# Blocks 2 and 3 on their way down: seven block products for eight, partial sums joined from SBUF, and first products that go on in the second's bank

## The chip, the cores and the metric

The kernel runs on one core of a Trainium2 chip. The metric is the device time of one execution in microseconds; lower is better. Engines are called as in the profile: PE is TensorE (with PEld, its weight loads), DVE is VectorE, ACT is ScalarE, POOL is GpSimd, SP is SyncE, whose queue issues the DMAs. Blocks, pairs and passes are counted from 0.

## What is computed

```python
for c in range(nc):                       # chunks of 32 queries, 16 keys more on the left, 8 on the right
    k_full = np.concatenate([mem_k, k[:, :, l_start:r_end]], axis=2)      # 8 memory keys
    v_full = np.concatenate([mem_v, v[:, :, l_start:r_end]], axis=2)
    scores = scale * np.matmul(q[:, :, c_start:c_end], k_full.transpose(0, 1, 3, 2))
    a = np.exp(scores - np.max(scores, axis=-1, keepdims=True))
    a = a / (np.sum(a, axis=-1, keepdims=True) + 1e-09)
    attn[:, :, c_start:c_end] = np.matmul(a, v_full)
x = attn.transpose(0, 2, 1, 3).reshape(3072, 512)       # batch 4, 8 heads, 768 tokens, 64 wide
h = x @ w_in                                            # 512 -> 2048
g = np.maximum(h, 0.0) + alpha * np.minimum(h, 0.0)
out = g @ w_out                                         # 2048 -> 512
```

## The kernel before

Everything is float32. A float32 product is made of three matmuls of a rounded type: each operand is kept as a high part (`xh`, `gh`) and a low part (`xl`, `gl`), and low x high, high x low and high x high add up in one PSUM bank. A high part is a cast on ScalarE, a low part a subtraction on VectorE ("split" below).

The 3072 tokens are eight blocks of 384 (`BT`), the 2048 features 16 slices of 128 (`NF`), the 512 inputs four parts of 128. A slice is multiplied upward into a bank `h_ps`, bent on ScalarE and VectorE (`g`), split, and multiplied downward into `o_ps`. Attention runs between these products in twelve events: score products `s_ps`, softmax on VectorE, ScalarE and POOL (`e`), eight transposes on VectorE (`pt`), value products `a_ps`.

- Blocks 0 and 1 go plainly (`hidden`): 12 upward matmuls of 384 columns a slice, 9 downward of 512 columns with the activations as the stationary operand.
- Blocks 2 and 3 go plainly for slices 0 to 7. Block 2's partial sum is put aside in HBM (`put_aside`), block 3's stays in its banks.
- Pass 0 (`whole`) takes slices 8 to 15 of blocks 2 and 3. Upward, two token blocks times two slices times two halves of the input make eight block products; sums of blocks of `x` and of the weights turn them into seven (a Strassen-Winograd scheme). Downward it multiplies plainly again, onto block 3's banks and into new ones for block 2, to which the part put aside is added (`put`).
- Passes 1 and 2 (`deep`) take blocks 4 and 5, then 6 and 7, with all 16 slices in eight pairs. They use seven products upward and downward: six matmuls of 384 columns a product. The sums of activations (`less`) are POOL's, the splits VectorE's (`gs`), the results are collected by `begun` (first part, copied out of the bank) and `ended` (second part, added).

The weights' sums are made by POOL, ScalarE and VectorE, split, stored to HBM (`w_all`, `w_two`) and loaded again before each product into a ring of ten slots (`w_p`) by SP's queue. `w_low` holds slices 0 to 7 of `w_out` plainly for passes 1 and 2. `make` builds the combinations of blocks 2 and 3 for pass 0, `transform` those of a later pass.

No engine's order is written down as such: each operation is a `step` with a cost, what it reads and writes, and a rank (`rest`, the work that still follows). A list scheduler fixes the order of every engine before the run; `MOVED` shifts the rank of single steps. An engine works its list in order, so what stands behind a waiting operation waits too.

Of the kernel before, what the change touches and what calls it, by code (L numbers as in the profile page):

```python
# [47 lines left out]
def first_slice(p):  # L48
    return 0 if p else PLAIN


# [3 lines left out]

NTT = BT // P
NPW, NPROD = NF // 2, 7
# [42 lines left out]
for f in range(NF):  # L100
# [6 lines left out]
PAIR, PASS, SHORT, DUO = 4.7, 134.0, 78.0, 15.7  # L107

DEEP = 1
DEEP_PASS = 119.0  # L110
BEHIND = SHORT + (DEEP - 1) * PASS + (NPASS - DEEP) * DEEP_PASS

BEGIN = (19, 24, 28, 31, 36, 41)


LAST_BEGINS = ((0, 4), (0, 6), (0, 7), (1, 24), (1, 47), (1, 74), (1, 96))
# [3 lines left out]
MAKE = 40  # L120

EVENT_LEAD = 8.0
# [4 lines left out]
STARTS_LONG = [x + 1 for x in BEGIN if x >= FIRST_LONG - 1] + [len(ORDER)]  # L127
# [5 lines left out]
FIRST_SUMS, SUMS_PACE = 21, 3.5  # L133
SUMS_ORDER = (0, 4, 5, 6, 7, 3, 1, 2)
SAVE_ORDER = (3, 1, 2, 4, 5, 6, 7, 0)
FIRST_SAVE, EARLY_SAVES = 23, 6
LOAD_AHEAD = 20.0

OVER = 2


LEAD = 9.5
# [8 lines left out]
DUE_WEIGHTS = 4  # L151
# [142 lines left out]
def body(ctx: ExitStack, tc: tile.TileContext, qvw, kw, first, w_in, w_out, alpha, out, out_t):  # L294
# [66 lines left out]
    def begins(u):  # L361

        if u < NWIN:
            return u // NPAIR
        n = (u - NWIN) // 2
        if n < len(BEGIN):
            return BEGIN[n]
        p, x = LAST_BEGINS[n - len(BEGIN)]
        lead = DUO * (min(x, NPW) - first_slice(p) // 2) + 2.1 * max(0, x - NPW - first_slice(p))
        return len(ORDER) + (BEHIND - pass_start(p) + lead) / PAIR  # L370
# [435 lines left out]

    OKEYS = [("o", i) for i in range(NTT)]
    ROOMS = {"gh0": (0, None), "gl0": (1, 0), "gh1": (1, 1)}
# [17 lines left out]
    def hidden(blk, f, first_f, last_f):  # L826
# [5 lines left out]
        if place >= BEGIN[0] + 3:  # L832
            hk = ("h0", "h1", "a")[place % 3]
# [57 lines left out]

        def down(o_ps):
# [24 lines left out]
        def add_down(o_ps, rank=None, after=()):  # L917
            step(PE, 0.697 * NTT, partial(down, o_ps), reads=[("w", 1, f, 0), ("w", 1, f, 1), gh, gl],
                 writes=[("s", 0), ("s", 1), "a"] if joint else OKEYS,
                 rest=rest(down_at) if rank is None else rank, after=after)  # L920
# [38 lines left out]
    aside = hbm.tile([P, NTT * DM], F32, name="aside")  # L959

    def put_aside(blk, o_ps):

        for tt in range(NTT):
            n = NTT + next(ntmp) % 2
            o = {}

            def take(tt=tt, n=n, o=o):
                o["t"] = tmp.tile([P, DM], F32, name="o_t", tag=f"o{n}")
                nc.scalar.copy(out=o["t"], in_=o_ps[tt])

            def leave(tt=tt, o=o):
                nc.sync.dma_start(out=aside[:, tt * DM:(tt + 1) * DM], in_=o["t"])

            step(ACT, 0.59, take, reads=OKEYS, writes=[("tmp", n)], rest=rest(PLACE[blk, PLAIN - 1] + 1))
            step(SP, 0.75, leave, reads=[("tmp", n)], writes=[("aside", tt)])

    def bring_back():

        for n in range(4):
            k, x = 2 + n // 2, "hl"[n % 2]  # L980

            def load(n=n, k=k, x=x):
                t = home(("aside", n), lambda: xp.tile([P, BT], F32, name="part", tag=f"x{x}{k}{AT[k][2]}"))
                nc.sync.dma_start(out=t, in_=aside[:, n * BT:(n + 1) * BT])

            step(SP, 0.65, load, reads=[("aside", tt) for tt in range(NTT)], writes=[("part", n)],
                 after=[("x" + x, k, AT[k][2])], rest=pass_start(1) + 6.0)

# [5 lines left out]
    w_low = hbm.tile([NPW, P, 2 * DM], F32, name="w_low")  # L994
    staged = {}

    def keep_plain(q):
# [8 lines left out]

        def whole(f):
            nc.sync.dma_start(out=w_low[f].rearrange("p (x m) -> p x m", x=2), in_=ws[f, 1].bitcast(F32))

        if q >= NPW // 2:  # L1010
            for f in (f1 - NPW, f2 - NPW):
                step(SP, 1.3, partial(whole, f), reads=[("w", 1, f, 0), ("w", 1, f, 1)], writes=[("wl", f)])
# [4 lines left out]
    def keep_sums(q):  # L1017
# [21 lines left out]
        def low(n, i):  # L1039
            nc.gpsimd.tensor_tensor(out=staged["x"][n][:, 1], in0=part(i),  # L1040
                                    in1=staged["x"][n][:, 0].bitcast(F32), op=ALU.subtract)
# [22 lines left out]
        def end(j, i):  # L1064
            n = spots[j]
            step(POOL, 0.75, partial(low, n, i), reads=[("sm", i)], writes=[("sx", n)])
            step(SP, 0.65, partial(leave, n, j), reads=[("sx", n)], writes=[("wd", q, j)])
# [42 lines left out]
    def raw_after(p, k, t):  # L1110
# [3 lines left out]
        part = [("part", (k - 2) * 2 + t)] if p == 2 and k >= 2 else []  # L1114
        return [("x" + key[1], key[2], AT[key[2]][2])] + part
# [59 lines left out]
    def combo(p, j, kt, x):  # L1175
# [16 lines left out]
    def combo_after(p, j, kt, x):  # L1192
        if p == 0:
            f = PLAIN + ((MADE[j] * 2 + kt) * 2 + x) // 2
            return [("w", 0, f, y) for y in range(2)]
        f = 2 + ((j * 2 + kt) * 2 + x) // 5
        old = [("raw7", k) for k in range(NK)] if f == LAST_SLOT else [("g0", 14), ("g0", 15)] if f == SPARE else []
        return [("w", i, f, y) for i in range(2) for y in range(2)] + old
# [5 lines left out]
    def load_product(q, j, left, kind="wd"):  # L1204
# [7 lines left out]
        def load():  # L1212
            t = home(("ring", k), room)
            wring[r] = t[:, n]
            if low:
                nc.sync.dma_start(out=t[:, n].bitcast(F32),
                                  in_=w_low[f].rearrange("p (x m) -> p x m", x=2)[:, :, i * HALF:(i + 1) * HALF])
            else:
                nc.sync.dma_start(out=t[:, n].rearrange("p x m -> p (x m)").bitcast(F32),
                                  in_=(w_all if kind == "wd" else w_two)[q, j])  # L1220

        low = kind == "w2" and q < NPW // 2 and j in QUARTERS
        if low:
            f, i = 2 * q + QUARTERS[j][0], QUARTERS[j][1]
        step(SP, 0.65, load, reads=[("wl", f) if low else (kind, q, j)], writes=[("wr", r)],
             after=[] if isinstance(k, str) else [("w", k[1], k[0], 0), ("w", k[1], k[0], 1)], rest=left)
        return r

    def load_low(f):
        _, at_ = out_place(f)  # L1230

        def load():
            nc.sync.dma_start(out=ws[at_, 0].rearrange("p x m -> p (x m)").bitcast(F32), in_=w_low[f])

# [131 lines left out]
    def whole(p):  # L1366
# [185 lines left out]
        for d in late:  # L1552
            down(o1, ob, *d)
# [502 lines left out]
```

## Time and profile before

| | |
|---|---|
| time, median of 3 runs | 569.68 us (569.61 to 570.16) |
| the profiled execution | 569.56 us |
| its span on the core | 567.8 us |
| TensorE busy | 561.1 us, 99% of the span |
| VectorE, ScalarE, POOL busy | 436.8, 337.9, 301.5 us |
| granted TensorE clock | 1.00 in every stage (the level of 2.4 GHz) |
| DMA, mean over the span | 267 GB/s |

The profiled execution is 0.12 us below the median; its time is its span and 1.8 us around it. Stages, in us from the span's start: blocks 0 and 1 with the plain halves of 2 and 3 up to 243.1, pass 0 to about 317.4 (with some steps beyond), pass 1 upward to 384.5 and downward to 447.8, pass 2 upward to 506.0 and downward to 564.4.

### The profile page before, as it was taken

Reading aid. Unit: us, or ns where it says so; the run is one execution under the profiler, and the core shown is the slowest. Engines: PE = TensorE matmul, PEld = TensorE weight load, DVE = VectorE, ACT = ScalarE, POOL = GpSimd, SP = SyncE. Lnnn points to the kernel's source line nnn. Section 1 sums busy time; section 2 is a strip of 40 time slices with the busy share of each in tenths; the row PEclk is TensorE's granted clock in tenths of the full one; section 3 lists DMA queues with packets and bytes.
Section 4 is the critical chain, followed back from the end, with each engine's and each line's share of the span. In section 5 each row is a group of like instructions: output and inputs, shape, how many; then the busy total and the mean of one; then the engine's idle time right before and its main releaser. Section 6 shows DMA issues by size and latency. Waiting matters only on the chain.

```text
span 567.8 us, 14440 instructions
## 1 busy us (share of the span) xinstructions
PE 561.1 (99%) x5356; PEld 520.4 (92%) x5356; DVE 436.8 (77%) x732; ACT 337.9 (60%) x912; POOL 301.5 (53%) x350
## 2 busy tenths in 40 slices
PE   8999999999999999999999999999999999999997
PEld 5889899888989888989998899999999999999997
DVE  4888899984849668767593897799999677669951
ACT  3798888664653466646755766766386255555540
POOL 3530000069889799998886992218935022229400
PEclk9999999999999999999999999999999999999999
DMA  8999998456476358377997799889887987878784
GB/s 344 398 407 408 409 352 295 152 179 194 155 253 227 103 164 293 126 269 240 319 321 284 216 349 327 291 281 289 257 274 223 321 270 252 255 248 258 234 291 141
DMA packets 82342, 151.44 MB, mean 267 GB/s; under 512 B 8416, under 2 KB 29408, under 8 KB 82272
## 3 DMA queue, kind: packets, MB, share of 16 engines
q1 hardware_dynamic: 82272, 150.51, 78.1%
q8 instruction: 43, 0.70, 0.5%
q14 instruction: 27, 0.22, 0.1%
HBM read 112.99 MB, written 37.49 MB: 265 GB/s over the span
## 4 chain that ended last, share of the span: by engine, by line
PE 96%; DMA 3%; issue 0%; DVE 0%; SPq 0%
PE h_ps L1713 21%; PE o_ps L1816 21%; PE h_ps L869 18%; PE o_ps L898 18%; PE o_ps L1438 6%; PE h_ps L1381 5%; PE a_ps L549 3%; DMA early<-first 3%; PE s_ps L451 3%; PE a_ps L701 1%; PE o_ps L687 1%; PE s_ps L427 0%; DVE o_t L1842 0%; SPq L623 0%
## 5 line engine op out<-in xcount | busy, mean ns | idle before, releaser
L1713 PE MATMUL h_ps<-xs,w_p 128*128 128x384 f32 x672 | 118.6, 335 | 0.0
L1779 POOL TENSOR_TENSOR big<-big 128x384 f32<-128x384 f32 x64 | 73.5, 1177 | 84.1 <-DVE big L1737 75.1
L1713 PEld LDWEIGHTS h_ps<-xs,w_p 128*128 128x128 f32 x672 | 116.5, 188 | 0.8
L1816 PE MATMUL o_ps<-gs,w_p 128*128 128x384 f32 x576 | 102.4, 335 | 0.0
L1816 PEld LDWEIGHTS o_ps<-gs,w_p 128*128 128x128 f32 x576 | 100.0, 188 | 0.2
L869 PE MATMUL h_ps<-xh,w 128*128 128x384 f32 x384 | 97.9, 335 | 0.0
L1801 DVE TENSOR_TENSOR gs<-big,gs 128x384 fp32r<-128x384 f32 x96 | 82.0, 893 | 8.6 <-ACT gs L1798 8.1
L510 POOL TENSOR_TENSOR e<-e,den 128x384 f32<-128x384 f32 x24 | 23.9, 1016 | 101.2 <-DVE den L506 98.6
L869 PEld LDWEIGHTS h_ps<-xh,w 128*128 128x128 f32 x384 | 69.6, 188 | 1.0
L1798 ACT CAST gs<-big 128x384 fp32r<-128x384 f32 x96 | 48.8, 522 | 28.7 <-PE o_ps L1816 24.6
L869 PE MATMUL h_ps<-xl,w 128*128 128x384 f32 x192 | 65.7, 342 | 0.0
L531 DVE STREAM_TRANSPOSE pt<-e 32x384 f32<-32x384 f32 x96 | 54.6, 569 | 7.0 <-POOL e L510 5.3
L484 ACT ACTIVATE e<-s_ps,mx 128x64 f32<-128x64 f32 x144 | 43.9, 336 | 12.3 <-DVE mx L477 12.3
L898 PE MATMUL o_ps<-w,gh 128*128 128x512 f32 x156 | 48.6, 393 | 0.0
L898 PE MATMUL o_ps<-w,room 128*128 128x512 f32 x165 | 45.2, 393 | 0.0
L898 PE MATMUL o_ps<-w,gl 128*128 128x512 f32 x111 | 43.8, 395 | 0.0
L878 ACT ACTIVATE g<-h_ps 128x384 f32<-128x384 f32 x48 | 23.8, 498 | 33.5 <-PE h_ps L869 23.3
L869 PEld LDWEIGHTS h_ps<-xl,w 128*128 128x128 f32 x192 | 36.0, 188 | 2.0
L881 DVE SCALAR_TENSOR_TENSOR g<-g,rise,h_ps 128x384 f32<-128x384 f32 x48 | 28.9, 607 | 11.3 <-ACT g L878 10.8
L1721 ACT COPY big<-h_ps 128x384 f32<-128x384 f32 x48 | 23.2, 483 | 22.2 <-PE h_ps L1713 20.9
L898 PEld LDWEIGHTS o_ps<-w,room 128*128 128x128 f32 x165 | 30.8, 188 | 6.1
L1734 ACT ACTIVATE g<-h_ps 128x384 f32<-128x384 f32 x48 | 23.6, 494 | 18.9 <-DVE h_ps L1724 14.3
(139 smaller groups left out, 1084.9 us busy)
## 6 DMA issues: line engine op xcount, KB each, us to landing
w_p<-w_all SPq DMA_DIRECT2D x140, 256.0 KB, 3.8
w_p<-w_two SPq DMA_DIRECT2D x88, 256.0 KB, 3.2
v_t<-qvw SPq DMA_DIRECT2D x24, 384.0 KB, 4.4
w_t<-w_in SPq DMA_DIRECT2D x16, 512.0 KB, 10.1
w_t<-w_out SPq DMA_DIRECT2D x16, 512.0 KB, 9.4
w_all<-sums_x SPq DMA_DIRECT2D x32, 256.0 KB, 3.8
w_two<-two_x SPq DMA_DIRECT2D x32, 256.0 KB, 4.2
qk<-kw SPq DMA_DIRECT2D x24, 272.0 KB, 4.1
```

The source lines that it names most:

```text
L484: nc.scalar.activation(out=st["e"][:, i], in_=st["s"][h2][:, n], func=AF.Exp, scale=SCALE, bias=d["mx"][:, u - us[0], n, h2:h2 + 1], accum ...
L531: nc.vector.transpose(out=pt[row:row + CH, g % 2], in_=e_pair.rearrange("p u n k -> p (u n) k")[g * CH:(g + 1) * CH, :, half * CH:(half + ...
L869: nc.tensor.matmul(out=h["ps"][:, :BT], lhsT=ws[f, 0][:, wk, k * P:(k + 1) * P], rhs=ring[k][xk][AT[k][blk]], start=(k == 0 and n == 0), s ...
L881: nc.vector.scalar_tensor_tensor(out=h["g"], in0=h["g"], scalar=rise[:, f:f + 1], in1=h["ps"][:, :BT], op0=ALU.mult, op1=ALU.add)
L898: nc.tensor.matmul(out=o_ps[tt], lhsT=h[gk][:, tt * P:(tt + 1) * P], rhs=ws[f, 1][:, wk], start=(f == first_f and i == 0), stop=(f == last ...
L1381: nc.tensor.matmul(out=t[0][:, :BT], lhsT=wring[r][:, wk, kt * P:(kt + 1) * P], rhs=combo(p, j, kt, xk), start=first and kt == 0 and n == ...
L1438: nc.tensor.matmul(out=o[tt], lhsT=d[gk][:, tt * P:(tt + 1) * P], rhs=w[:, wk], start=f == (first_slice(p) if o is o2 else 0) and n == 0, ...
L1713: nc.tensor.matmul(out=t["t"][:, :BT], lhsT=wring[r][:, wk, kt * P:(kt + 1) * P], rhs=combo(p, j, kt, xk), start=first and kt == 0 and n = ...
L1779: step(POOL, 1.02, lambda: nc.gpsimd.tensor_tensor(out=quad(q, dst), in0=quad(q, a), in1=quad(q, b), op=ALU.subtract), reads=[key(q, a), k ...
L1798: nc.scalar.copy(out=hi(), in_=quad(q, i))
L1801: nc.vector.tensor_tensor(out=lo(), in0=quad(q, i), in1=hi().bitcast(F32), op=ALU.subtract)
L1816: nc.tensor.matmul(out=t["t"][:, :BT], lhsT=wring[r][:, wk, dd * P:(dd + 1) * P], rhs=parts[xk](), start=first and q == 0 and n == 0, stop ...
```

## The change

`whole` is gone, and `deep` serves pass 0 too, with pairs 4 to 7 alone (`first_pair`), so that slices 8 to 15 of blocks 2 and 3 go downward by seven products for eight. For this their slices 0 to 7 go downward with the weights as the stationary operand (`down_turned`): 12 matmuls of 384 columns a slice into four banks, the result turned. Block 2's partial sum goes to HBM in four pieces of 384 columns, block 3's is kept in SBUF (`keep_part`), and pass 0's `begun` and `ended` add the banks to both.

In every pass a first product that others build on is copied by ScalarE from its bank X into bank Y (`passed`), and the next product adds to Y in PSUM, where VectorE added a copy before; the order of the downward products changes for this. Ten operations of `make` and eight low parts of weight sums go from POOL to VectorE, the weights' sums are made in another order, `w_low` goes away, and the tables that place the attention's events and the moved steps are new.

```diff
+def first_pair(p):
+    return 0 if p else PLAIN // 2
...
-LAST_BEGINS = ((0, 4), (0, 6), (0, 7), (1, 24), (1, 47), (1, 74), (1, 96))
+LAST_BEGINS = ((0, 1), (0, 22), (0, 46), (1, 27), (1, 68), (1, 86), (1, 106))
...
-EVENT_LEAD = 8.0
+EVENT_LEAD = 24.0
...
+LOW_OUT = (0, 5)
+MAKE_DVE = (1,)
...
+        def down_turned(o_ps):
+            if f == first_f:
+                o_ps.extend(bank_tile(k, "o_ps") for k in TKEYS)
+            for fb in range(NFB):
+                for i, (wk, gk) in enumerate(((0, "gl"), (1, "gh"), (0, "gh"))):
+                    nc.tensor.matmul(
+                        out=o_ps[fb][:, :BT],
+                        lhsT=ws[f, 1][:, wk, fb * P:(fb + 1) * P],
+                        rhs=h[gk],
+                        start=(f == first_f and i == 0), stop=(f == last_f and i == 2),
+                    )
...
+    def keep_part(o_ps, clock):
+
+        for fb in range(NFB):
+            def take(fb=fb):
+                (nc.vector.tensor_copy if fb % 2 else nc.scalar.copy)(out=first_tile(4 * NPW + fb), in_=o_ps[fb][:, :BT])
...
+                (nc.vector if kt in MAKE_DVE else nc.gpsimd).tensor_tensor(out=rooms[r][0](), in0=get(a), in1=get(b), op=alu)
...
-    DOWN_ORDER = (0, 1, 2, 3, 5, 4, 6)
+    DOWN_ORDER = (0, 2, 3, 1, 4, 5, 6)
...
+        def passed(t, to, name):
+            def go():
+                to["t"] = bank_tile(to["k"], name)
+                nc.scalar.copy(out=to["t"][:, :BT], in_=t["t"][:, :BT])
+
+            act(0.48, go, [t["k"]], [to["k"]])
+
...
-                    if j == 0:
+                    if j == 0 and opening:
                         copied(t[i], q, 0)
+                    elif j == 0:
+                        passed(t[i], y[i], "h_ps")
                     elif j == 1:
-                        added(t[i], q, 0, True)
+                        if opening:
+                            added(t[i], q, 0, True)
                         bent(f1, q, 0, t[i])
...
-            first = j in (0, 1, 2, 6)
+            first = j in (0, 2)
...
+            if p == 0:
+                fb = i // 2 * 2 + d
+                k = ("part" if i % 2 else "p3", fb)
+
+                def join():
+                    t = o["t"] = homes[k] if i % 2 else first_tile(4 * NPW + fb)
+                    nc.vector.tensor_tensor(out=t, in0=bank[j][d]["t"][:, :BT], in1=t, op=ALU.add)
+
+                o = held[i, d] = {"k": k}
+                dve(0.56, join, [bank[j][d]["k"]], [k])
+                return
...
-                    if j in (0, 2, 3):
-                        begun(j, d, {0: 0, 2: 3, 3: 1}[j])
-                    elif j == 4:
-                        ended(j, d, 3)
-                        begun(j, d, 2)
-                    else:
-                        ended(j, d, {1: 0, 5: 1, 6: 2}[j])
+                    if j in (0, 4):
+                        passed(X[d], Y[d], "o_ps")
+                    if j in (1, 2, 3, 6):
+                        begun(j, d, {1: 0, 2: 3, 3: 1, 6: 2}[j])
+                    if j in (4, 5):
+                        ended(j, d, {4: 3, 5: 1}[j])
+                    elif j in (1, 6):
+                        leaves(d, {1: 0, 6: 2}[j])
```

What this does to the order is seen at three places. The first is TensorE at the end of pass 0. Before, L1438 is the plain downward product of pass 0 (9 matmuls of 512 columns a slice) and L1713 pass 1's upward product:

```order
L1438 MATMUL o_ps<-w,gl 128x512
L1438 MATMUL o_ps<-w,gh 128x512 x2
L451 MATMUL s_ps<-qk_162 32x64 x24
L451 MATMUL s_ps<-qk_163 32x64 x24
L1438 MATMUL o_ps<-w,gs 128x512 x9
L1713 MATMUL h_ps<-xs,w_p 128x384 x12
```

After, L1609 is the downward product and L1487 the upward one of all passes (`made` is an operand of pass 0, `xs` of pass 1):

```order
L1609 MATMUL o_ps<-gs,w_p 128x384 x6
L1487 MATMUL h_ps<-made,w_p 128x384 x6
L1609 MATMUL o_ps<-gs,w_p 128x384 x132
L549 MATMUL a_ps<-pt,v_t 64x32 x48
L1487 MATMUL h_ps<-xs,w_p 128x384 x6
L1609 MATMUL o_ps<-gs,w_p 128x384 x6
L1487 MATMUL h_ps<-xs,w_p 128x384 x12
L1609 MATMUL o_ps<-gs,w_p 128x384 x6
L1487 MATMUL h_ps<-xs,w_p 128x384 x6
```

The value products `a_ps` of an event now stand behind 22 downward products in a row and ahead of the last of pass 0, which alternate with pass 1's first.

The second place is VectorE ahead of those value products, which need the last transposes (L531) of this piece. After the change (L1594 is a split, L1627 an addition of a bank to a partial sum, L1518 a bend):

```order
L1518 SCALAR_TENSOR_TENSOR big<-g,rise,h_ps 128x384
L1594 TENSOR_TENSOR gs<-big,gs 128x384 x8
L531 STREAM_TRANSPOSE pt<-e 32x384
L1594 TENSOR_TENSOR gs<-big,gs 128x384 x2
L1627 TENSOR_TENSOR part<-o_ps,part 128x384 x4
L1594 TENSOR_TENSOR gs<-big,gs 128x384 x4
L531 STREAM_TRANSPOSE pt<-e 32x384
L1594 TENSOR_TENSOR gs<-big,gs 128x384
L1627 TENSOR_TENSOR big<-o_ps,big 128x384
L1594 TENSOR_TENSOR gs<-big,gs 128x384
L531 STREAM_TRANSPOSE pt<-e 32x384 x6
```

Before, VectorE's list has at the end of pass 0 the splits of the plain way down (L1425) and pass 1's first operands (L1312):

```order
L1425 TENSOR_TENSOR gl<-g_3617,gh 128x384
L1425 TENSOR_TENSOR gl<-g_3546,gh 128x384
L1425 TENSOR_TENSOR gs<-g_3952,gs 128x384
L1312 TENSOR_TENSOR xs<-raw,xs 128x384
L1425 TENSOR_TENSOR gl<-g_3952,gh 128x384
L1312 TENSOR_TENSOR xs<-raw,xs 128x384 x3
```

The splits of the new way down and the additions to the partial sums have come in between the transposes.

The third place is ScalarE in a pass's upward products. Before, pass 1 has only copies into SBUF there (L1721), here with splits' high parts (L1798) and a cast of a weights' sum (L1597) around them:

```order
L1597 CAST two_x<-two 128x256
L1798 CAST gs<-big 128x384
L1721 COPY big<-h_ps 128x384
L1798 CAST gs<-big 128x384
L1721 COPY big<-h_ps 128x384
L1597 CAST two_x<-two 128x256
```

After, in pass 0, the copies from bank to bank (L1500) stand with bends' first parts (L1515), splits' high parts (L1591) and copies into SBUF (L1495):

```order
L1500 COPY h_ps<-h_ps 128x384 x2
L1515 ACTIVATE g<-h_ps 128x384
L1591 CAST gs<-big 128x384
L1495 COPY big<-h_ps 128x384
L1591 CAST gs<-big 128x384
L1495 COPY big<-h_ps 128x384
```

A copy of the first product stands where one stood before, but its target is now the bank that the next product writes.

## Rows read from the trace of the kernel before

**Rows 1.** The page, busy time of each engine, its share of the span, its instructions.

```profile
PE 561.1 (99%) x5356; PEld 520.4 (92%) x5356; DVE 436.8 (77%) x732; ACT 337.9 (60%) x912; POOL 301.5 (53%) x350
```

**Rows 2.** Waits of TensorE: its line, what it waited for, us in total, times, longest.

```profile
PE s_ps L413 <- DVE warm L347: 1.5, 1, 1.5
PE a_ps L701 <- DMA early<-first: 0.9, 1, 0.9
PE s_ps L451 <- issue: 0.6, 2, 0.4
PE s_ps L427 <- DMA early<-first: 0.3, 1, 0.3
```

**Rows 3.** Windows: length, then PE, PEld, DVE, ACT, POOL busy, clock, DMA share, GB/s.

```profile
243.10:317.40 74.30, 73.91 (x899) 65.41 (x898) 50.58 (x87) 43.53 (x141) 62.61 (x77) 1.00 0.85 286
...
384.50:447.80 63.30, 63.30 (x627) 62.38 (x626) 60.77 (x89) 35.13 (x104) 37.78 (x32) 1.00 0.83 259
```

**Rows 4.** The chain that ended last, in order of time: start, us, what, instructions.

```profile
39.03 2.10 PE h_ps L869 x12
...
49.51 4.12 PE o_ps L898 x18
...
185.09 10.24 PE o_ps L898 x45
...
447.77 58.24 PE h_ps L1713 x336
...
564.38 0.56 DVE o_t L1842
```

**Rows 5.** Timeline of VectorE: start, first start to last end, line, operation, count.

```profile
339.43 1.03 DVE L1724 TENSOR_TENSOR h_ps<-h_ps,big 128x384 f32<-128x384 f32 x2
384.02 1.13 DVE L1737 SCALAR_TENSOR_TENSOR big<-g,rise,h_ps 128x384 f32<-128x384 f32 x2
390.00 0.23 DVE L506 RECIPROCAL den<-den 128x12 f32<-128x12 f32 x1
393.52 4.67 DVE L531 STREAM_TRANSPOSE pt<-e 32x384 f32<-32x384 f32 x8
405.13 10.49 DVE L1801 TENSOR_TENSOR gs<-big,gs 128x384 fp32r<-128x384 f32 x10
430.00 4.55 DVE L1801 TENSOR_TENSOR gs<-big,gs 128x384 fp32r<-128x384 f32 x6
434.47 2.67 DVE L1801 TENSOR_TENSOR five<-big,five 128x384 fp32r<-128x384 f32 x2
437.06 3.59 DVE L1801 TENSOR_TENSOR gs<-big,gs 128x384 fp32r<-128x384 f32 x4
440.57 1.01 DVE L1842 TENSOR_TENSOR o_t<-o_ps,o_t 128x384 f32<-128x384 f32 x2
517.97 14.25 DVE L1801 TENSOR_TENSOR gs<-big,gs 128x384 fp32r<-128x384 f32 x11
534.48 2.88 DVE L1801 TENSOR_TENSOR gs<-big,gs 128x384 fp32r<-128x384 f32 x6
```

**Rows 6.** POOL: timeline from 397 us; group of pass 0 (busy, mean ns).

```profile
397.35 13.88 POOL L1779 TENSOR_TENSOR big<-big 128x384 f32<-128x384 f32 x11
...
L1594 POOL TENSOR_TENSOR two<-two 128x256 f32<-128x256 f32 x10 | 8.0, 805 | 0.2
```

**Rows 7.** Timeline of TensorE and ScalarE at pass 2's beginning.

```profile
447.61 4.67 PE L1713 MATMUL h_ps<-xs,w_p 128*128 128x384 f32 x26
448.85 0.48 ACT L1721 COPY big<-h_ps 128x384 f32<-128x384 f32 x1 [8.25 <-PE h_ps L1713]
449.89 0.48 ACT L1721 COPY big<-h_ps 128x384 f32<-128x384 f32 x1 [0.56 <-PE h_ps L1713]
```

**Rows 8.** DMA issues of the page: queue, count, KB each, us to landing.

```profile
w_p<-w_all SPq DMA_DIRECT2D x140, 256.0 KB, 3.8
w_p<-w_two SPq DMA_DIRECT2D x88, 256.0 KB, 3.2
```

More of the change, by code (lines that the diff above doesn't have):

```diff
@@ L149 @@
 NLESS = 4
-DUE_WEIGHTS = 4
+DUE_WEIGHTS = 3
 SLACK = 2.5
@@ L917, in add_down @@
         def add_down(o_ps, rank=None, after=()):
-            step(PE, 0.697 * NTT, partial(down, o_ps), reads=[("w", 1, f, 0), ("w", 1, f, 1), gh, gl],
-                 writes=[("s", 0), ("s", 1), "a"] if joint else OKEYS,
-                 rest=rest(down_at) if rank is None else rank, after=after)
+            step(PE, 0.697 * NTT, partial(down if blk < 2 else down_turned, o_ps),
+                 reads=[("w", 1, f, 0), ("w", 1, f, 1), gh, gl],
+                 writes=([("s", 0), ("s", 1), "a"] if joint else OKEYS if blk < 2 else TKEYS) + list(after),
+                 rest=rest(down_at) if rank is None else rank)
         return add_up, add_bend, add_down
@@ L957, in send @@
         nc.sync.dma_start(out=out[row:row + P, :], in_=o["t"])
-    aside = hbm.tile([P, NTT * DM], F32, name="aside")
+    aside = hbm.tile([NFB, P, BT], F32, name="aside")
     def put_aside(blk, o_ps):
-        for tt in range(NTT):
+        for fb in range(NFB):
             n = NTT + next(ntmp) % 2
             o = {}
[L967 to L975, printed above, removed]
@@ L977, in bring_back, with take @@
-    def bring_back():
[L979 to L987, printed above, removed]
+            def take(fb=fb, n=n, o=o):
+                o["t"] = tmp.tile([P, BT], F32, name="o_t", tag=f"o{n}")
+                nc.scalar.copy(out=o["t"], in_=o_ps[fb][:, :BT])
@@ new lines, in leave, with part_tag, load @@
+            def leave(fb=fb, o=o):
+                nc.sync.dma_start(out=aside[fb], in_=o["t"])
+            step(ACT, 0.48, take, reads=[TKEYS[fb]], writes=[("tmp", n)], rest=rest(PLACE[blk, PLAIN - 1] + 1))
+            step(SP, 0.65, leave, reads=[("tmp", n)], writes=[("aside", fb)])
+    def part_tag(fb):
+        return "hl"[fb % 2], 2 + fb // 2
+    def bring_back():
+        for fb in range(NFB):
+            x, k = part_tag(fb)
+            def load(fb=fb, k=k, x=x):
+                t = home(("part", fb), lambda: xp.tile([P, BT], F32, name="part", tag=f"x{x}{k}{AT[k][3]}"))
+                nc.sync.dma_start(out=t, in_=aside[fb])
+            step(SP, 0.65, load, reads=[("aside", fb)], writes=[("part", fb)], after=[("x" + x, k, AT[k][3])])
@@ L991, in body @@
+    def keep_part(o_ps, clock):
+        for fb in range(NFB):
+            def take(fb=fb):
+                (nc.vector.tensor_copy if fb % 2 else nc.scalar.copy)(out=first_tile(4 * NPW + fb), in_=o_ps[fb][:, :BT])
+            step(*((DVE, 0.56) if fb % 2 else (ACT, 0.48)), take, reads=[TKEYS[fb]], writes=[("p3", fb)],
+                 after=slot_free(first_slot(4 * NPW + fb)), rest=clock)
     HALF = DM // 2
@@ L1852, in deep @@
             work = []
-            for q in range(NPW):
+            for q in range(first_q, NPW):
                 sums(j, q)
@@ L1974, in body, with over, go @@
         if PLACE[blk, f] == MAKE:
+            for q in SAVE_ORDER[:EARLY_SAVES]:
+                save_plain(q)
+                save_sums(q)
             make()
-    overs += [down, lambda rank: None]
-    banks_left = OKEYS + ["h0", "h1", "a"] if DEEP == 1 else ["h0", "h1", "a"] + OKEYS
-    for q in SAVE_ORDER[:-1]:
-        if q >= NPW // 2:
-            save_plain(q)
+    overs.append(down)
+    last_block = o_ps[NBLK - 1, PLAIN]
+    def over(part):
+        def go(clock):
+            part(rank=clock[0], after=seq(0))
+            clock[0] -= 2 * TICK
+        return go
+    overs[:] = [over(part) for part in overs] + [lambda clock: keep_part(last_block, clock[0])]
+    for q in SAVE_ORDER[EARLY_SAVES:]:
+        save_plain(q)
         save_sums(q)
+    banks_left = ["h0", "h1", *TKEYS]
     for p in range(NPASS):
```

413 lines of the change are left out of this document (103 added, 310 removed), and 7 rows, old and new, of the table MOVED.

## The prediction

> **What bounds the kernel now.** I read the engine totals first, then who waits for whom, then the stages, then the single rows. The totals name TensorE: busy 99% of the span, with VectorE next at 77% [rows 1]. The waits show that this 99% is work and not waiting behind something: TensorE's idle time is 2.7 us in two early places and 0.6 us of issue [rows 2]. So the time falls only if TensorE gets less to do, and it rises with every wait that another engine gives it. The stages say where that could be. In the present pass 0 (243.1 to 317.4 us) VectorE is busy 50.6 of 74.3 us and POOL 62.6; in pass 1's way down (384.5 to 447.8 us) VectorE is busy 60.8 of 63.3 us, and TensorE still does not wait [rows 3]. The change gives pass 0 a way down of that second kind, while POOL's work of the first kind is still there. That is the place to cost.
>
> **TensorE's part: what is removed and added.** Before, the downward products of blocks 2 and 3 are 2 x 16 slices x 9 matmuls = 288 of 512 columns. After, their first eight slices take 2 x 8 x 12 = 192 of 384 columns (`down_turned`), and their second eight 28 products of 6 = 168, also of 384. The prices come from the chain of waits, where TensorE's stretches stand with their counts [rows 4]. 512 columns: (10.24 - 4.12) / (45 - 18) = 0.2267 us, with 0.04 us more per unbroken run (4.12 - 18 x 0.2267). 384 columns: 58.24 / 336 = 0.1733 us, with 0.02 us per run (2.10 - 12 x 0.1733). Sum: -288 x 0.2267 + 360 x 0.1733 = -65.29 + 62.39 = -2.90 us. By the order of TensorE's instructions the 512-column runs go from 42 to 21 and the 384-column ones from 61 to 74: -0.84 + 0.26 us. Together **-3.5 us**. The upward products and the attention's matmuls are as many as before. The profiled execution took 569.56 us, so a TensorE that is kept busy gives 566.1 us, or 566.2 beside the median (569.68, 0.12 above the profiled one).
>
> **The copies from bank to bank.** `passed` lets ScalarE copy a first product from bank X into bank Y, and the next product goes on in Y. Before, TensorE started into Y at once and VectorE added afterwards. 18 of the upward copies are tight: between the end of a pair's product and its next one lies only the other pair's product, 6 x 0.1733 = 1.04 us. The timeline shows the chain: TensorE starts at 447.61, the product ends 1.04 later, the copy begins at 448.85, so the hop is 0.20; the copy takes 0.48 [rows 7]. With a like hop back that is 0.88 us of 1.04. I cost it at nothing; its cover is that ScalarE does nothing longer than 0.16 us in front. The two copies leave 0.56 us between them [rows 7], room for one short activation. If another of 0.48 stands in front, a copy is 0.3 late; 18 times that is 5.8 us, the upper end. The 12 downward copies have at least four products, 4.2 us, of room. The 16 VectorE additions that go away save nothing by themselves, since TensorE did not wait for them, and neither do the `ended` ones; at the very end the last operation is a copy in place of a 0.56 us addition [rows 4]: -0.1.
>
> **VectorE in the new pass 0.** This is the term that decides. I count in the order of instructions from the moment that TensorE ends product 4 of pair 6 (the seventh pair). From there to the third attention event's value products (`a_ps`) TensorE has 3 products, then four in alternation with two late upward ones among them, then 22: 29 products, 29 x 1.04 = 30.2 us. In the same time VectorE must do what stands ahead of that event's last transposes: 4 additions, 6 bends, the reciprocal's pair, 5 joins (the new `begun` additions to the partial sums), 8 transposes and 19 splits (`gs<-big,gs`). TensorE can take nothing from behind: its order is fixed.
>
> Back to back, these cost their spacing, not their duration, since the next begins before the last one ends [rows 5]: additions 1.03 / 2, some 0.48 after the first, bends 0.53, joins 0.47, transposes 4.67 / 8 = 0.58, the reciprocal 0.23 and its partner taken as the same, less overlap 0.4. So 4 x 0.48 + 6 x 0.53 + 0.4 + 5 x 0.47 + 8 x 0.58 = 12.5 us, and with the hop 12.7. The 19 splits remain, at c each. TensorE waits once 12.7 + 19 c is over 30.2, that is from **c = 0.92**.
>
> What c is hangs on POOL. Alone, six splits take 2.88 us, 0.48 each. Beside an unbroken row of POOL's subtractions (11 in 13.88 us [rows 6]) ten take 10.49, 1.05 each, and in the worst piece eleven take 14.25, 1.30 each. With POOL on for part of the time, twelve from 430.00 to 440.65 take 0.89 each [rows 5]. Both inputs of a split lie in SBUF. Additions, joins and four of the six bends have one in PSUM; I leave all of them at the prices above.
>
> The Trainium skill, "SBUF — State Buffer", section "Who interferes with whom", says that a VectorE instruction with two SBUF inputs and a GpSimd instruction that reads SBUF exclude each other for a whole instruction. By that rule each of the 19 could have to wait out a whole POOL operation before its own 0.48 us, which is the strict case among the rivals. The pieces at 405 and 518 us [rows 5] agree that the two hinder each other, but at 1.05 to 1.30 for one split, so the sum goes by the rows.
>
> POOL in this stretch has 16 operations 384 wide (10 of them the new pass-0 subtractions, `less`) and 13 of 256 columns (sums for the weights), where a 256-wide one takes 0.81 [rows 6]: about 16 x 1.26 + 13 x 0.8 = 31 us of a stretch of 32, but some of it while VectorE transposes, bends and joins. The first ten splits meet the unbroken subtractions (1.05), the other nine a mixture (0.89 to 1.05). I take **c = 1.0**: VectorE is ready at 31.7, TensorE waits 1.5 us. Both ends stay: 0.48 gives nothing, 1.30 gives 37.4 - 30.2 = 7.2.
>
> Behind the event there is a little more. Four further splits and six `xs` lows stand between additions, while TensorE alternates `o_ps` products that need these splits with pass 1's first products. By the same spacings VectorE is behind by 0.0, 0.1, 0.0 and 0.5 us at the four: **+0.5**. What waits behind the stalled value products is everything of TensorE, so these 2.0 us go straight into the end.
>
> **Edits with no price.** `keep_part` (2 copies each on ScalarE and VectorE), `put_aside` and `bring_back` in four 384-wide pieces, ten of `make`'s operations and eight lows moved from POOL to VectorE lie where VectorE is not full; none of them costs more than a 384-wide POOL operation's 1.26 [rows 6], and that cover is what they need. The queue on SP loses the `w_low` traffic and gets 28 more weight loads and twelve quarter stores. In pass 0 that is some 44 loads and 13 stores of 256 KB plus the attention's, about 17 MB in 48 us, 360 GB/s. Loads land 3.2 to 3.8 us after issue [rows 8] and ten slots lie ahead, so I cost them at nothing; pass 0 moved 286 GB/s before [rows 3].
>
> Sum: 569.56 - 3.5 - 0.1 + 1.5 + 0.5 = 568.0, beside the median **568.1 us**, 0.3% faster.
>
> **Rivals.** *TensorE stays covered* (c under 0.92, as 430 to 440 us shows): 566.1 to 566.6 us; against it stands POOL's load in the stretch. *It cancels*: at c = 1.06 to 1.15, VectorE is ready at 32.8 to 34.6 and the waits are 3.1 to 4.9, so 569.2 to 571.0; its lower half is no change. *Slower, by POOL*: c = 1.15 to 1.30 as in the row of eleven, waits of 4.9 to 7.7, **571.0 to 573.8 us**. It decides from c = 1.15 on; for it speaks that the `less` results are themselves due (the late splits wait for them), against it that 13 of POOL's 29 are short. *Strict alternation*: every split first waits out one of POOL's 29 operations, 31 / 29 = 1.07 us on average, so c = 1.55, VectorE is ready at 42.2 and the time is 578; against it stands that no piece of eleven splits reached it. *The bank copies stall*: up to 5.8 us on top, 572 where VectorE's own wait is nothing; ScalarE's 60% of busy time speaks against more than a few of the 18. *SP's queue lags*: the 17 MB at pass 0's 286 GB/s would take 60 us for 48; ten loads ahead are worth 10 us, so 2 us, 568.2 without VectorE's wait.
>
> **How the numbers follow.** Covered 0.24; the main case with c between 0.92 and 1.06: 0.30; cancelling 0.2; slower by POOL 0.15; strict alternation 0.01; copies 0.06; queue 0.04. What a measurement here can tell from no change is 0.2%, 1.14 us: faster is under 568.5, slower above 570.8. Faster takes all of the first, most of the main case, and the queue: 0.52. No change takes the rest of the main case and most of the cancelling one: 0.23. Slower: 0.25. The range reaches from the covered case, 565.9, to 572.2, which leaves out the worst of POOL and copies. The likeliest case's own range is 566.3 to 569.3.
>
> **What would show it.** TensorE's matmuls sum to 3.5 us less. A wait of about 1.5 us on `a_ps` L549 for VectorE's transposes at the end of pass 0, with small ones on `o_ps` L1609 behind it, and no others. The splits (L1594) of that stretch at about 1.0 us each, with POOL over 85% busy. No waits on `h_ps` L1487 for ScalarE's L1500. I am wrong if the splits there stand 0.9 apart or less (no wait, 566), or 1.15 and more (5 us of wait), or if waits appear at L1487.

## The result and the profile after

The changed kernel takes 574.81 us (573.82 to 575.53, six runs), the kernel before 569.64 in the same set: ratio 1.0088, 95% interval 1.0075 to 1.0101. It is 0.9% slower; 568.1 was forecast, and 574.81 lies above the range. The profiled execution took 574.60 us, 572.5 of them its span.

Engine totals of the page, against [rows 1]:

```profile
PE 561.5 (98%) x5428; PEld 529.6 (93%) x5428; DVE 448.1 (78%) x744; ACT 349.2 (61%) x936; POOL 311.9 (54%) x348
```

TensorE's busy time did not fall, although it has less to do. The waits of its weight loads show more than those of its matmuls: a matmul of 384 columns is drawn 0.33 us long though the next begins 0.17 us after it, and one behind a stall longer still (0.44 us at 216.91). The larger ones that a release on another engine ends and that [rows 2] has nothing of:

```profile
PEld h_ps L870 <- DVE g L882: 2.4, 4, 1.1
PEld o_ps L1609 <- DVE gs L1594: 2.4, 2, 2.1
...
PEld o_ps L898 <- ACT o_t L983: 1.0, 1, 1.0
PEld o_ps L1609 <- DVE part L1627: 0.9, 1, 0.9
...
PEld h_ps L1487 <- ACT h_ps L1500: 0.7, 2, 0.4
```

So there are two places, and the windows put them in time (columns as in [rows 3]):

```profile
200.00:245.60 45.60, 43.38 (x505) 41.09 (x506) 38.59 (x67) 26.59 (x100) 43.36 (x50) 1.00 0.66 220
...
299.00:312.50 13.50, 11.14 (x61) 10.19 (x60) 13.39 (x18) 7.08 (x17) 13.50 (x14) 1.00 0.87 281
312.50:330.80 18.30, 18.26 (x271) 17.61 (x271) 17.36 (x25) 10.23 (x26) 16.39 (x17) 0.91 0.83 270
```

The first lies in the plain halves of blocks 2 and 3, at 215 to 225 us; in the window around it POOL is busy 43.4 of 45.6 us. The second is the end of pass 0, where VectorE and POOL have no gap left. Behind it the granted clock is under 1.00, which it was nowhere before.

**Pass 0's end.** TensorE's timeline of the changed kernel, from the 22 downward products of pass 0 that stand in a row (132 matmuls) to the event's value products:

```profile
289.34 14.28 PE L1609 MATMUL o_ps<-gs,w_p 128*128 128x384 f32 x78
304.23 6.53 PE L1609 MATMUL o_ps<-gs,w_p 128*128 128x384 f32 x36 [0.61 <-DVE part L1627]
312.54 4.96 PE L1609 MATMUL o_ps<-gs,w_p 128*128 128x384 f32 x18 [1.78 <-DVE gs L1594]
317.43 1.60 PE L549 MATMUL a_ps<-pt,v_t 64*64 64x32 f32 x96
```

TensorE is held before the products, not before `a_ps` as forecast, and the 18 matmuls behind the longest stall take 4.96 us. The same 18 behind a like stall in the profiled execution of e14 (below) take 3.40:

```profile
313.88 3.40 PE L1609 MATMUL o_ps<-gs,w_p 128*128 128x384 f32 x18 [1.80 <-DVE gs L1594]
```

The windows of the changed kernel show where the other 1.6 us come from:

```profile
311.00:313.00 2.00, 0.46 (x3) 0.46 (x4) 1.99 (x5) 0.00 (x0) 2.00 (x2) 1.00 0.85 277
313.00:315.00 2.00, 2.00 (x10) 2.00 (x10) 1.92 (x4) 1.42 (x4) 2.00 (x4) 0.69 0.70 244
315.00:317.00 2.00, 2.00 (x8) 2.00 (x7) 1.72 (x4) 0.74 (x3) 2.00 (x3) 0.50 0.56 146
317.00:319.00 2.00, 2.00 (x100) 1.69 (x98) 1.77 (x5) 0.44 (x2) 0.77 (x2) 0.96 0.57 159
```

After a stretch in which TensorE worked 0.46 of 2 us, the granted clock went to 0.50, the level of 1.2 GHz, and from 317 us on it was back at 0.96. Such a stall isn't always followed by a fall: in e14's execution the clock stayed at 1.00. In the two runs of the changed kernel whose mean clock is 1.000 the span is 571.8 and 572.0 us, in the four with 0.997 it is 572.5 to 573.4; those two still take 573.82 and 574.10 us, so the clock is not the main part of the loss.

VectorE in the same stretch, against [rows 5]:

```profile
292.00 1.86 DVE L1594 TENSOR_TENSOR gs<-big,gs 128x384 fp32r<-128x384 f32 x2
294.02 1.12 DVE L1594 TENSOR_TENSOR gs<-big,gs 128x384 fp32r<-128x384 f32 x1 [0.16 <-ACT gs L1591]
295.31 5.63 DVE L1594 TENSOR_TENSOR gs<-big,gs 128x384 fp32r<-128x384 f32 x5 [0.17 <-ACT gs L1591]
300.97 0.57 DVE L531 STREAM_TRANSPOSE pt<-e 32x384 f32<-32x384 f32 x1
301.57 1.68 DVE L1594 TENSOR_TENSOR gs<-big,gs 128x384 fp32r<-128x384 f32 x2
303.17 1.94 DVE L1627 TENSOR_TENSOR part<-o_ps,part 128x384 f32<-128x384 f32 x4
305.03 4.21 DVE L1594 TENSOR_TENSOR gs<-big,gs 128x384 fp32r<-128x384 f32 x4
...
311.61 0.88 DVE L1594 TENSOR_TENSOR gs<-big,gs 128x384 fp32r<-128x384 f32 x1
312.41 3.51 DVE L531 STREAM_TRANSPOSE pt<-e 32x384 f32<-32x384 f32 x6
```

Five splits stand 1.13 apart, four 1.05. Beside them POOL works without a gap, on subtractions, weight sums and the softmax, all of which read SBUF. The last split ends at 312.49, and TensorE's product begins at 312.54.

**At 215 to 225 us.** What ScalarE waited for from 186 to 246 us:

```profile
ACT two_x L1360 <- POOL two L1357: 8.2, 6, 2.2
ACT gh L887 <- DVE g L882: 5.1, 4, 1.8
ACT made L1251 <- POOL one L1244: 2.5, 2, 1.6
```

ScalarE's list holds the bends' first part (L879) and the copies of block 2's banks (`put_aside`, L983) behind casts of POOL's sums (L1360) and of pass 0's operands (L1251). Three times the bend or the copy comes late to TensorE, for 1.13, 0.84 and 1.00 us of its weight loads, 3.0 us in all. The second and the third stall are as simple as that: ScalarE waits for POOL, and what TensorE needs stands next in its list.

```profile
218.05 0.51 ACT L1251 CAST made<-one 128x384 fp32r<-128x384 f32 x1 [1.55 <-POOL one L1244]
218.47 0.49 ACT L879 ACTIVATE g<-h_ps 128x384 f32<-128x384 f32 x1
...
223.05 0.40 ACT L1360 CAST two_x<-two 128x256 fp32r<-128x256 f32 x1 [0.61 <-POOL two L1357]
223.36 0.47 ACT L983 COPY o_t<-o_ps 128x384 f32<-128x384 f32 x1
```

The first runs through VectorE too. Ahead of the bend ScalarE has the softmax's twelve exponentials (L484). ScalarE came to them late, since a cast had waited 2.2 us for a POOL sum, and then waited 0.18 us more for VectorE's maximum (L477). That stood behind operations of `make` that the change had moved to VectorE, of 1.05 to 1.11 us each beside POOL's (0.55 in e3):

```profile
209.57 1.11 DVE L1244 TENSOR_TENSOR x_t<-x_t,xl 128x384 f32<-128x384 f32 x1
210.60 0.71 DVE L477 TENSOR_SCALAR mx<-mx 128x12 f32<-128x12 f32 x1
...
211.40 0.32 ACT L484 ACTIVATE e<-s_ps,mx 128x64 f32<-128x64 f32 x1 [0.18 <-DVE mx L477]
...
214.90 0.92 ACT L983 COPY o_t<-o_ps 128x384 f32<-128x384 f32 x2
215.63 0.58 ACT L879 ACTIVATE g<-h_ps 128x384 f32<-128x384 f32 x1
```

From 186 to 230 us VectorE is busy 40.3 of 44 us, in the kernel before 30.6. POOL is busy 43.9 there, but before the change it was at 41.6 already, and TensorE did not wait:

```profile
186.00:230.00 44.00, 44.00 (x576) 39.11 (x575) 30.59 (x53) 24.01 (x90) 41.64 (x45) 1.00 0.55 185
```

```profile
186.00:230.00 44.00, 41.98 (x582) 39.80 (x582) 40.31 (x64) 25.15 (x85) 43.92 (x47) 1.00 0.54 176
```

The first of these windows is the kernel before, the second the changed one.

### The profile page after: what moved, and what is told of

Its sections match the earlier page's. It is cut to its first block, busy times and chain, and to the rows that moved or that the text cites. A ratio compares the mean times of both kernels' runs of the same rounds, so it can differ in the third digit from the quotient of the medians.

```text
span 572.5 us, 14645 instructions
## 1 busy us (share of the span) xinstructions
PE 561.5 (98%) x5428; PEld 529.6 (93%) x5428; DVE 448.1 (78%) x744; ACT 349.2 (61%) x936; POOL 311.9 (54%) x348
## 4 chain that ended last, share of the span: by engine, by line
PE 86%; DMA 4%; POOL 4%; DVE 4%; issue 1%; ACT 1%; SPq 0%; POOLq 0%
PE h_ps L1487 25%; PE o_ps L1609 23%; PE h_ps L870 15%; PE o_ps L911 12%; PE o_ps L898 4%; DMA early<-first 3%; PE a_ps L549 3%; PE s_ps L451 2%; DVE gs L1594 1%; DVE xs L1282 1%; PE a_ps L701 1%; POOL sums L1049 1%; POOL sums_x L1055 1%; POOL two_x L1363 1%; PE o_ps L687 1%
## 5 line engine op out<-in xcount | busy, mean ns | idle before, releaser
L1609 PE MATMUL o_ps<-gs,w_p 128*128 128x384 f32 x744 | 135.8, 339 | 2.4 <-DVE gs L1594 1.8
L1572 POOL TENSOR_TENSOR big<-big 128x384 f32<-128x384 f32 x80 | 90.0, 1149 | 83.8 <-DVE big L1518 57.3
L1609 PEld LDWEIGHTS o_ps<-gs,w_p 128*128 128x128 f32 x744 | 130.6, 190 | 4.0 <-DVE gs L1594 2.4
L1487 PE MATMUL h_ps<-xs,w_p 128*128 128x384 f32 x672 | 118.7, 335 | 0.1
L1487 PEld LDWEIGHTS h_ps<-xs,w_p 128*128 128x128 f32 x672 | 116.4, 188 | 0.7 <-ACT h_ps L1500 0.4
L1594 DVE TENSOR_TENSOR gs<-big,gs 128x384 fp32r<-128x384 f32 x124 | 99.3, 825 | 16.2 <-ACT gs L1591 15.6
L870 PE MATMUL h_ps<-xh,w 128*128 128x384 f32 x384 | 97.9, 335 | 0.0
L1591 ACT CAST gs<-big 128x384 fp32r<-128x384 f32 x124 | 62.3, 518 | 36.4 <-PE o_ps L1609 27.0
L870 PEld LDWEIGHTS h_ps<-xh,w 128*128 128x128 f32 x384 | 69.6, 188 | 0.8
L870 PE MATMUL h_ps<-xl,w 128*128 128x384 f32 x192 | 66.2, 345 | 1.3 <-DVE g L882 1.3
L531 DVE STREAM_TRANSPOSE pt<-e 32x384 f32<-32x384 f32 x96 | 54.6, 569 | 3.3 <-POOL e L510 1.7
L1357 POOL TENSOR_TENSOR two<-w 128x256 f32<-128x256 f32 x24 | 21.6, 908 | 56.6 <-DVE w L787 56.6
L484 ACT ACTIVATE e<-s_ps,mx 128x64 f32<-128x64 f32 x144 | 43.4, 333 | 9.8 <-DVE mx L477 9.7
L1518 DVE SCALAR_TENSOR_TENSOR big<-g,rise,h_ps 128x384 f32<-128x384 f32 x60 | 35.6, 606 | 7.9 <-ACT g L1515 6.9
L911 PE MATMUL o_ps<-w,room 128*128 128x512 f32 x150 | 41.0, 392 | 0.0
L1515 ACT ACTIVATE g<-h_ps 128x384 f32<-128x384 f32 x60 | 29.6, 494 | 17.3 <-PE h_ps L1487 8.0
L870 PEld LDWEIGHTS h_ps<-xl,w 128*128 128x128 f32 x192 | 36.0, 188 | 4.3 <-DVE g L882 2.4
L879 ACT ACTIVATE g<-h_ps 128x384 f32<-128x384 f32 x48 | 23.9, 501 | 22.9 <-PE h_ps L870 16.0
L882 DVE SCALAR_TENSOR_TENSOR g<-g,rise,h_ps 128x384 f32<-128x384 f32 x48 | 29.0, 606 | 5.3 <-ACT g L879 5.2
L484 ACT ACTIVATION_READ_ACCUMULATOR e<-s_ps,mx 128x1 f32 x144 | 32.3, 224 | 0.0
```

Source lines behind the costliest of these rows:

```text
L484: nc.scalar.activation(out=st["e"][:, i], in_=st["s"][h2][:, n], func=AF.Exp, scale=SCALE, bias=d["mx"][:, u - us[0], n, h2:h2 + 1], accum ...
L531: nc.vector.transpose(out=pt[row:row + CH, g % 2], in_=e_pair.rearrange("p u n k -> p (u n) k")[g * CH:(g + 1) * CH, :, half * CH:(half + ...
L870: nc.tensor.matmul(out=h["ps"][:, :BT], lhsT=ws[f, 0][:, wk, k * P:(k + 1) * P], rhs=ring[k][xk][AT[k][blk]], start=(k == 0 and n == 0), s ...
L882: nc.vector.scalar_tensor_tensor(out=h["g"], in0=h["g"], scalar=rise[:, f:f + 1], in1=h["ps"][:, :BT], op0=ALU.mult, op1=ALU.add)
L911: nc.tensor.matmul(out=o_ps[tt], lhsT=h[gk][:, tt * P:(tt + 1) * P], rhs=ws[f, 1][:, wk], start=(f == first_f and i == 0), stop=(f == last ...
L1487: nc.tensor.matmul(out=t["t"][:, :BT], lhsT=wring[r][:, wk, kt * P:(kt + 1) * P], rhs=combo(p, j, kt, xk), start=first and kt == 0 and n = ...
```

## The experiments

Each time stands beside runs of the kernel before on the same chip in the same set.

**Thinning, with the order of every engine unchanged.** e1:

```diff
-lambda: nc.gpsimd.tensor_tensor(out=quad(q, dst), in0=quad(q, a), in1=quad(q, b),
+lambda w=BT if p else 8: nc.gpsimd.tensor_tensor(out=quad(q, dst)[:, :w], in0=quad(q, a)[:, :w], in1=quad(q, b)[:, :w],
```

> The changed kernel with the 16 subtractions that POOL makes for pass 0's downward products (L1572, p = 0) done on 8 of 384 columns; order of every engine unchanged. Theory A (VectorE is the bound of pass 0's end, and POOL's subtractions make its splits long): a split falls from about 1.05 to 0.75 us apart, VectorE is ready 5 us earlier, TensorE's 3 us of waits at the end of pass 0 and the lower clock behind them go: 570.5 to 571. Theory B (TensorE waits there for the weights that SP's queue brings; the chain names a w_p load of 2.3 us): no change, 574 to 575.5.

Measured: 570.92 us (570.71 to 571.47), 1.0027 (1.0016 to 1.0039) of the kernel before.

e2:

```diff
-nc.vector.tensor_tensor(out=lo(), in0=quad(q, i), in1=hi().bitcast(F32), op=ALU.subtract)
+nc.vector.tensor_tensor(out=lo(), in0=quad(q, i), in1=hi().bitcast(F32), op=ALU.subtract) if p else nc.vector.memset(lo().bitcast(F32), 0.0)
```

> The changed kernel with the 28 splits' low parts of pass 0 (VectorE, L1594, p = 0) replaced by a fill with zeros, which reads nothing; POOL's work unchanged. Theory A: VectorE loses some 25 us of work at the end of pass 0, the waits there go: 570.5 to 571, and the 2.2 us of waits at 215 to 225 us stay. Theory B (weights or POOL's own lateness): 574 to 575.5.

Measured: 570.30 us (569.01 to 571.58), 1.0014 (1.0003 to 1.0025).

e3 (the lows likewise):

```diff
-nc.gpsimd.tensor_tensor(out=part(dst), in0=get(a), in1=get(b), op=alu)
+nc.gpsimd.tensor_tensor(out=part(dst)[:, :8], in0=get(a)[:, :8], in1=get(b)[:, :8], op=alu)
```

> The changed kernel with all of POOL's weight sums and their low parts (L1049, L1055, L1357, L1363) done on 8 columns. Theory A with a second part (POOL, busy 95% from 186 to 245 us, also delays the making of pass 0's operands and through ScalarE's queue the copies out of block 2's banks): both places free, 568 to 569. If only pass 0's end hangs on POOL: 570.5 to 571 with the waits at 215 to 225 us still there. Theory B: 574 to 575.5.

Measured: 568.28 us (567.40 to 568.92), 0.9979 (0.9969 to 0.9988).

e5, the three together:

> The three thinnings at once: pass 0's subtractions and all weight sums on 8 columns, pass 0's splits filled with zeros; order unchanged. It shows what TensorE's own work is worth once nothing holds it. If the count of the prediction (3.5 us less matmul time) is right and no third place waits: 566.0 to 566.8, 2.6 to 3.4 under before. If the turned downward product or the interleaved order costs TensorE more than counted: 567.5 or above, with its waits gone.

Measured: 566.70 us (566.23 to 568.89), 0.9958 (0.9946 to 0.9970).

Theory A holds and B falls: less work of POOL or less of VectorE takes away TensorE's waits for VectorE at pass 0's end, all but 0.4 to 0.5 us, with the weights' loads untouched. In e1 the splits of the stretch are shorter, where 1079 ns is the changed kernel's mean. First the changed kernel, then e1, both from 282.3 to 316 us:

```profile
L1594 DVE TENSOR_TENSOR gs<-big,gs 128x384 fp32r<-128x384 f32 x19 | 19.8, 1079 | 1.3 <-ACT gs L1591 1.2
```

```profile
L1594 DVE TENSOR_TENSOR gs<-big,gs 128x384 fp32r<-128x384 f32 x20 | 13.2, 682 | 4.1 <-ACT gs L1591 4.0
```

e1 has a new wait instead, 1.0 us (1.4 of the weight loads) on a bank copy in pass 0's way up, behind a ScalarE cast that waited 1.2 us for a store. e1 and e2 keep the waits at L870 and L898; e3 has none of them, so POOL's weight sums made those too. Whether they did it by being late themselves or by slowing VectorE isn't parted: in e3 VectorE's 67 operations from 200 to 245.6 us take 30.4 us in place of 38.6, and no run relieves VectorE alone there. e5 gives what TensorE's part of the change is worth: 2.75 us less than before in one set.

e10, the control on the kernel before (the same thinning as e3):

> A control: the kernel before with all of POOL's weight sums and their low parts on 8 columns; order unchanged. If it is the change that made POOL's work a bound, nothing changes here, since TensorE did not wait: 569.2 to 569.8. If POOL held the kernel before too: 567.5 to 568.5.

Measured: 569.14 us (568.86 to 570.16), 0.9994 (0.9985 to 1.0003). POOL did not hold the kernel before, though it was nearly as full; only the change made its work count.

**What lengthens a split.** e9, in pass 0 in place of POOL's subtraction:

```diff
+(lambda: [nc.gpsimd.memset(quad(q, dst), 0.0) for _ in range(3)])
```

> The changed kernel with each of pass 0's 16 subtractions on POOL replaced by three fills of the same tile with zeros, which read nothing from SBUF but keep POOL occupied; order unchanged. If a split is lengthened only by a POOL operation that reads SBUF (as the Trainium skill's page SBUF — State Buffer, section Who interferes with whom, has it): the splits beside the fills fall to 0.48 us apart, and the time to 570.5 to 571.5 as with the subtractions thinned. If any POOL operation on SBUF lengthens them: as the changed kernel, 574 to 575.5.

Measured: 572.87 us (572.41 to 573.15), 1.0058 (1.0041 to 1.0075), between the two. VectorE of e9, and POOL beside it:

```profile
295.82 1.97 DVE L1594 TENSOR_TENSOR gs<-big,gs 128x384 fp32r<-128x384 f32 x4 [0.75 <-ACT gs L1591]
```

```profile
292.55 5.33 POOL L1573 MEMSET big<- 128x384 f32 x12
```

Four splits stand 0.49 apart while POOL fills without a gap; beside its reading operations five stood 1.13 apart. So it is a POOL operation that reads SBUF which lengthens a split, as the section of the Trainium skill's page "SBUF — State Buffer" that the prediction names has it. The time stays above e1's. Three fills last 1.33 us, no less than a subtraction (1.15 on average), and ScalarE's list waits for them as before: VectorE idles 4.6 us for ScalarE's casts from 282 to 318 us, and TensorE's weight loads wait 1.6 us for splits and joins and 2.5 us for bank copies (e1: 0.7 and 1.8).

**The bank copies.** e4:

```diff
                     elif j == 0:
-                        passed(t[i], y[i], "h_ps")
+                        copied(t[i], q, 0)
                     elif j == 1:
-                        if opening:
-                            added(t[i], q, 0, True)
+                        added(t[i], q, 0, True)
```

> The changed kernel with the 16 upward copies from bank to bank undone: the first product is copied to SBUF, the second starts its own bank and VectorE adds, as before the change. If the copies only cost what the rows show (two short waits of TensorE's weight loads, 0.7 us): 574.0 to 574.5. If they are what costs (0.3 us each): 570. If they are free and the 16 additions fall on a full VectorE: 575 to 576.

Measured: 575.39 us (574.82 to 576.29), 1.0106 (1.0091 to 1.0121). The trace shows all 18 upward copies undone (the expectation counts 16). Against the changed kernel's 1.0088 (1.0075 to 1.0101) the intervals overlap, so the copies are no loss here; without them TensorE's waits for splits grow from 1.8 to 3.6 us, and two of the additions fall into pass 0. They are not free in every order: e1 and e9 wait for them.

**Moving work from POOL to VectorE.** e6 sets `MAKE_DVE = (0, 1)`; e7 gives pass 0's subtractions to VectorE (`step(DVE, 0.56, ...)`); e8 does both. The scheduler places everything anew.

> The changed kernel with the other ten operations of make on VectorE too (MAKE_DVE = (0, 1)); the scheduler places everything anew. Theory A2 (POOL's fullness is what makes pass 0's operands and block 2's copies late): POOL has 11 us less at 186 to 245 us, the 2.2 us of waits there go, pass 0's end stays: 572 to 573. Rival (VectorE is what is late there, TensorE waits for its bend L882): ten more operations on VectorE make these waits longer, 575.5 to 577.

> The changed kernel with pass 0's 16 subtractions moved from POOL to VectorE; the scheduler places everything anew. By the spacings of the rows each costs VectorE 0.48 us and takes away the collision that lengthened a split by some 0.6, and ScalarE no longer waits for POOL: 571.5 to 573.5. Rival (VectorE is simply full and 16 more operations add 7.7 us to it): 577 or more.

> Both moves from POOL to VectorE together. If the two places are apart, the gains add: 569.5 to 571.5. If VectorE becomes the bound between them: no better than the better of the two alone.

Measured: 578.07 (577.03 to 578.91), 577.93 (576.76 to 578.69) and 579.32 us (578.51 to 579.66): 1.0152, 1.0148 and 1.0173. All three miss what I expected of A and go the rivals' way, e6 beyond its rival's 577. In e7 TensorE waits 2.1 us for the transposes, which the scheduler put at 318 us, behind pass 1's operands. To part the order from the amount, e13 to e15 move the same operations while the plan still counts them as POOL's (the edit of e13; e14 does the like with `make`, e15 both):

```diff
-lambda: nc.gpsimd.tensor_tensor(out=quad(q, dst), in0=quad(q, a), in1=quad(q, b),
+lambda: (nc.gpsimd if p else nc.vector).tensor_tensor(out=quad(q, dst), in0=quad(q, a), in1=quad(q, b),
```

> As e7 (pass 0's 16 subtractions on VectorE), but the scheduler still plans them for POOL, so that every other operation keeps its place. If e7 lost by its order: VectorE pays 0.48 us for each and gets back some 0.6 on a split, ScalarE no longer waits for POOL, the 3.3 us of waits at pass 0's end and the lower clock behind them mostly go: 571 to 572.5. If VectorE's amount is what holds it: 575 to 578, as e7.

> As e6 (all of make on VectorE), with every other operation in its place. If e6 lost by its order: the waits at 215 to 225 us go, 572 to 573.5. If VectorE's amount holds it: the waits there grow, 575.5 to 578.

> Both with the order kept. If both gain: 569 to 570.5, about as the kernel before. If VectorE's amount holds it: 576 or more.

Measured: 575.57 (573.71 to 577.73), 575.02 (574.66 to 575.92) and 575.54 us (574.50 to 578.39): 1.0103, 1.0094 and 1.0117. So of e6's and e8's loss some 3 us were the new order; for e7 (2.6 us) the intervals just touch. With the order kept nothing is gained: none of the three is told from the changed kernel, and e14 and e15 end half a microsecond under the range expected if VectorE's amount holds. In e13 splits and subtractions in turn stand 0.47 us apart from 295 to 298 us, while POOL idles, but VectorE has to pay for the operations it took over. In the orders tried, its amount of work is the bound there, and the collisions are only part of it; an order made for the moved operations isn't tested.

**Starting POOL's sums earlier.** `FIRST_SAVE` 16 and 12 for 19:

> The changed kernel with the sums of w_out allowed from the 16th slice on instead of the 19th (FIRST_SAVE = 16), so that POOL, which is idle for 70% of 34 to 140 us, has less left at the end of pass 0; the scheduler places everything anew. If POOL's backlog is what makes both waits: 571.5 to 574. Rival (VectorE's amount of work at pass 0's end holds it, and another order loses what the old one had): 575 to 578.

> The same with FIRST_SAVE = 12. POOL's backlog: 570 to 573. Rival: 575 to 578, or waits already in blocks 0 and 1, where VectorE is busy 88% and now shares with POOL.

Measured: 582.32 (581.69 to 584.76) and 581.87 us (579.47 to 584.05), 1.0232 and 1.0215, above every range I had expected. In both, TensorE waits in blocks 0 to 3 for splits and bends (L891, L882), 4 to 6 us, and still at pass 0's end. New order and earlier sharing aren't told apart here. No version that does the whole work beat the kernel before.

## Why the prediction was wrong

**TensorE's part: mostly right.** Counted -3.5 us; e5 gives -2.75 of medians. Of the difference 0.4 us is a wait between passes 1 and 2 that e5 has too: there ScalarE's copy into the bank comes late, behind casts that wait for POOL. The copies' cover was that ScalarE does nothing longer than 0.16 us in front of them; here a cast of 0.52 us and two copies of results stood there. Waits at L1487 were named as a sign of being wrong, and two came (0.7 us of weight loads).

**VectorE in the new pass 0: right place and price, wait too small.** c was taken as 1.0; the 19 splits stand 1.02 apart (19.4 us in all). What failed is that the sum went by VectorE's work alone. It left out 1.3 us in which VectorE waited, nearly all for ScalarE's high parts, which in part waited for POOL's subtractions (2.5 us of ScalarE's waits there). It set the deadline at `a_ps`, which waited for no transpose (they were done at 315.92), while TensorE was held earlier, at the products that need the splits and joins: 3.3 us of its weight loads (2.4 and 0.9). And it had no term for the clock: 4.96 - 3.40 = 1.6 us in this execution. From the first downward product of the piece (285.18 us) to the end of the event's scores the changed kernel takes 45.6 us, e5 40.7: 4.9 us where 2.0 were forecast. The +0.5 behind the event was nothing.

**"Edits with no price": the step that failed outright.** It took the moved operations to "lie where VectorE is not full" and put them at nothing. VectorE was nearly full where they came to lie: busy 40.3 of 44 us from 186 to 230 us. And I did not look at POOL, which makes the rest of pass 0's operands beside the weights' sums and has to be done earlier (last operation of `make` at 225.9 us, before at 234.1), while ScalarE's list ties the lateness of both engines to TensorE. Measured: 3.0 us at 215 to 225 us, gone in e3. How these divide between POOL's lateness and VectorE's load stays open. This place stood in no rival.

Together: 568.0 forecast for the profiled execution, + 3.0 + 2.9 + 0.4 and 0.4 at the start (its first load came later) = 574.7; it took 574.6. That it closes to 0.1 is partly luck: the time around the span, 2.1 us for 1.8 before, has no term in it. The rival "slower, by POOL" had the right direction and 571.0 to 573.8 us, but by c of 1.15 and more, which wasn't so. The bank copies and SP's queue stayed as costed, but for that 0.4.

## What to carry to other kernels

When an operation count falls on the engine that bounds the kernel, list for each stage what every other engine has to do in the shorter time, and go through the in-order lists: an engine that is half idle, here ScalarE, passes one engine's lateness on to another. Price a VectorE operation with both inputs in SBUF by what stands on POOL beside it (here 0.48 us alone, 1.05 to 1.13 beside operations that read SBUF); moving one from POOL to VectorE exchanges a collision for the operation itself. Cost the operations that you move, too, at the place where they come to lie. A short stall of TensorE can cost more than its length if the clock falls behind it (1.6 us here), but it need not (e14).

## What the runs showed of the hardware

A split next to POOL operations that read SBUF stood 1.05 to 1.13 us apart from the next, next to POOL fills 0.49, as alone (0.48 [rows 5]). After a stretch with TensorE busy 0.46 of 2 us the granted clock fell to 0.50 for part of 4 us; behind a stall of the same length in e14 (1.80 us for 1.78) it stayed at 1.00, and so it did in that stage in e1 to e3, where TensorE's waits for VectorE are 0.5 us or less.
